# A 1x1 memset instead of a no-operation ahead of each indirect addition of GpSimd

## The chip, the cores and the metric

One core of a Trainium2 chip runs the whole kernel. The metric is the device time of one execution in microseconds (us); a verdict compares medians of several executions. The engines are TensorE (PE, with its weight loads PEld), VectorE (DVE), ScalarE (ACT), GpSimd (POOL) and SyncE (SP), which only issues transfers here.

## The reference

The input is x (4 sequences of 3584 positions, 192 channels), 14336 tokens in all. First comes a causal convolution whose seven weights differ for every position and head and are a softmax over the seven taps:

```
w   = softmax(weight_gen, over 7 taps)          # 4 x 3584 x 8 heads x 7
a   = sum over k of w[..., h, k] * x_pad[s + k, head h]
```

Then a mixture of 8 experts on the 14336 rows `a`: noisy logits from two small products, the two largest of eight, softmax over these two, and for each chosen expert

```
out[row] += top2_w * (relu(a[row] @ w1[e]) @ w2[e])   # 192 -> 1024 -> 192
```

So every output row is the sum of two experts' rows, and these are added where they lie.

## The kernel before, in words

The tokens are cut into 14 chunks of 1024. For each chunk VectorE does the convolution (`conv`, L323 and L333 are its products and sums), ScalarE and VectorE split the rows into two float16 parts in a record buffer `rec` (`split`, L344 and L348), SyncE transposes them for the gate product (L370), and `routing` finds each token's two experts and its place in their queues. GpSimd then writes the records of the chunk to the queues in DRAM (`xg`) by 16 indirect DMAs of 128 rows each (`scatters`, `scatter`, L406 and L407: a 1x1 memset of the tile `spacer`, and the DMA).

Expert work runs in 15 rounds, 14 with blocks of 256 rows for each of the 8 experts and one with blocks of 128. For a round SyncE reads the rows' gates (`meta`, L794) and the transposed rows (`xT`, L800) from the queues (`prologues`). TensorE computes the first product of a block in steps of 512 columns (`mm1`, L856), ScalarE takes its relu (`hi`, L871), VectorE the float16 rest (`lo`, L875), TensorE the second product (`mm2`, L896). `finish` then scales the result into a buffer y on ScalarE (L908; there are six such buffers, four at first) and adds it into the output with an indirect DMA of GpSimd (L913): one addition for each 128 rows, 232 in all. An addition of one block waits until those of the block before have landed.

Nothing of the order is left to chance at run time: each engine has one queue, in the order in which a planner (`Sched`) emits the instructions. Every piece of work is a generator that yields the engine, a duration in us, the function that emits the instruction, and what it depends on. The planner keeps for each engine the time at which it is free. In `step` it takes the earliest piece that could start, and among the pieces of the same engine that could start within 0.3 us of it the one of highest priority. The duration only moves the planner's clock. The pieces this change touches or meets are

- the scatters: duration 1.5, priority 5;
- the additions: duration 1.4, priority 7.5, not before 2.0 us after y is planned to be ready;
- the first and second product: 1.09 and 1.04 for a step, four steps in a block of 256 rows;
- `T["add", n]` and `T["added", bi]`, the planner's times for a free buffer y and for a landed addition, which hang on the addition's planned end, and `T["queued", c]`, which hangs on the last scatter's and lets a round's loads be planned.

A loop at the end (`leftovers`) treats what the rounds left, with a no-operation and an addition of its own.

Of the kernel before, what the change touches and what calls it, by code (L numbers as in the profile page):

```python
# [36 lines left out]
ROUNDS = [(c, 256) for c in range(NC)] + [(NC - 1, 128)]  # L37
# [12 lines left out]
GL, AL, ML, UL, XL = 5.0, 2.0, 5.0, 15.0, 6.0  # L50
# [93 lines left out]
def moe_kernel(ctx, tc, x_lay, wgen, noise, wgn, w1, w2, xg, out):  # L144
    nc = tc.nc
# [27 lines left out]
    def act(n):  # L173
        return (n / 1.2 + 190) / 1e3
# [35 lines left out]
    spacer = const.tile([1, 1], F32, name="spacer")  # L210
# [21 lines left out]
    def before(key, i, n):  # L232

        return [(key, i - n)] if i >= n else []
# [518 lines left out]
    added = []  # L753
# [6 lines left out]
    for c, (_, b) in enumerate(ROUNDS):  # L760
        for e in range(E):
            o = Block()
# [5 lines left out]
    meta, gate_of, token = {}, {}, {}  # L768
# [130 lines left out]
    def finish(bi, t0):  # L899

        o = blist[bi]
        mine = []
        for t in range(o.nt):
            y = []

            def scale():
                y.append((blk if v < 4 else late[1]).tile([P, D], F32, name=f"y{v}", bufs=1))
                nc.scalar.activation(y[0], o.py[t // 2][:, (t % 2) * D:(t % 2 + 1) * D], AF.Copy,  # L908
                                     scale=gate_of[o.c][:, o.e, t:t + 1])

            def add():
                nc.gpsimd.nop()
                i = nc.gpsimd.indirect_dma_start(  # L913
                    out=out, out_offset=bass.IndirectOffsetOnAxis(ap=token[o.c][:, o.e, t:t + 1], axis=0),
                    in_=y[0], in_offset=None, compute_op=OP.add)
                for p in mine:
                    tc.declare_no_dep(i.ins, p.ins, reason="a token has one row in an expert's queue")
                mine.append(i)
                added.append(i)

            n = adds[0]
            adds[0] += 1
            v, u = take(ylast, YB if late else 4, n)
            ty = yield ("ACT", act(D) + 0.07, scale, [t0, ("g", o.c, o.e)] + ([("add", u)] if u is not None else []))
            if t == o.nt - 1:
                T["y", bi] = ty
            ta = yield ("POOL", 1.4, add, [ty + (AL if o.c else 0.0), ("clear", ROUNDS[o.c][0]), ("token", o.c)] + before("added", bi, 1), 0.27)
            T["add", n] = ta + 2.2
        T["added", bi] = ta + 2.6
        if o.e == E - 1:  # L930
            T["round", o.c] = ta + 2.6
# [4 lines left out]
    def take(last, n, user):  # L936

        v = min(range(n), key=lambda i: last.get(i, -1))
        u = last.get(v)
        last[v] = user  # L940
        return v, u
# [4 lines left out]
    def tensor():  # L946
# [3 lines left out]
        def second():  # L950
            sj = pend.pop(0)
            bj, s = steps[sj]
            o = blist[bj]
            deps = [("lo", sj), ("low2", o.e)] + (before("y", bj, 2) if s == 0 else [])
            T["mm2", sj] = t = yield ("PE", 1.04 * o.nf * o.b / 512, lambda: mm2(sj), deps)
            if s == o.n - 1:
                sch.spawn(finish(bj, t), 7.5)
# [155 lines left out]
```

## Time and profile before

| | us |
|---|---|
| median of 3 runs | 1298.4 (1297.04 to 1300.36) |
| the profiled execution | 1293.18 |
| its span, first to last instruction | 1291.4 |
| TensorE busy | 1101.0 |
| VectorE busy | 813.7 |
| GpSimd busy | 731.2 |
| ScalarE busy | 549.6 |

Busy times are those of one profiled execution. A group of instructions is a source line (L913), an engine, what it writes and reads, a count, the busy time and the mean of one. Idle time in front of an instruction is given with what released it; that is inferred from semaphore events. The granted clock (PEclk) is TensorE's, as a share of full speed.

### The profile page before, as it was taken

The page shows a single profiled execution, that of the slowest core. Times are in us where ns is not written, and L with a number is a line of the kernel's source. Part 1 is how long each engine was busy: PE and PEld are TensorE (multiplying, and loading weights), DVE is VectorE, ACT ScalarE, POOL GpSimd, SP SyncE. Part 2 cuts the span into 40 slices and gives each one's busy share as a digit, 9 for nine tenths or more (in the row PEclk, how much of TensorE's full clock was granted, in tenths as well). Part 3 has the DMA queues.
Part 4 walks back from the last instruction along what each step waited for, and adds up shares of the span by engine and source line. Part 5 has one row for each costly group of instructions (what it writes and reads, how often), then busy time and mean ns, then how long its engine had stood idle before and what let it go on. Part 6 is the DMA issues. An engine that isn't in the chain of part 4 may idle for free.

```text
span 1291.4 us, 27931 instructions
## 1 busy us (share of the span) xinstructions
PE 1101.0 (85%) x10958; PEld 975.8 (76%) x10958; DVE 813.7 (63%) x1540; ACT 549.6 (43%) x1231; POOL 731.2 (57%) x781
## 2 busy tenths in 40 slices
PE   0267999999969979889869889969799999999994
PEld 0033677988968969678859879869688889999994
DVE  5447858778868878677858778858644533333331
ACT  6587774444424334324333434323323333333331
POOL 0025165475876847658466574867756777333332
PEclk9998998999999999889989999989898999999997
DMA  9952585537536475455564737546273544334331
GB/s 254 300 164 57 113 203 81 124 75 142 111 58 147 125 98 125 75 104 128 89 126 73 144 65 137 113 60 101 51 102 68 89 82 78 45 50 48 38 39 20
DMA packets 249686, 132.49 MB, mean 103 GB/s; under 512 B 182096, under 2 KB 242000, under 8 KB 247888
## 3 DMA queue, kind: packets, MB, share of 16 engines
q1 hardware_dynamic: 205392, 85.37, 30.3%
q0 software_dynamic: 44160, 45.31, 22.5%
q8 instruction: 86, 1.41, 0.5%
q14 instruction: 48, 0.39, 0.1%
HBM read 38.70 MB, written 58.10 MB: 75 GB/s over the span
## 4 chain that ended last, share of the span: by engine, by line
PE 67%; issue 7%; DMA 7%; ACT 5%; DVE 5%; POOL 4%; SPq 3%; another core or an unknown queue 1%; ACTq 0%; POOLq 0%; DVEq 0%
PE pm L856 34%; PE py L896 29%; POOL xg L407 3%; DMA out<-y,token 2%; PE sums L715 2%; ACT junk L269 2%; DMA xt<-x_lay 2%; SPq L794 1%; POOL out L913 1%; DVE acc L333 1%; DVE tmp L323 1%; DMA xg<-rec,pos 1%; SPq L370 1%; DMA xT<-xg 1%
## 5 line engine op out<-in xcount | busy, mean ns | idle before, releaser
L856 PE MATMUL pm<-xT,wres 128*128 128x256 f16 (+1 forms) x4800 | 601.9, 273 | 27.9 <-DMA xT<-xg 17.9
L913 POOL DMA_INDIRECT out<-y,token x232 | 407.6, 1757 | 364.5 <-ACT y L908 175.2
L896 PE MATMUL py<-wres,hi 128*128 128x192 f16 x3712 | 509.7, 249 | 48.7 <-ACT y L908 18.4
L875 DVE SCALAR_TENSOR_TENSOR lo<-pm,hi 128x512 f16<-128x512 f32 x464 | 316.5, 687 | 345.6 <-ACT hi L871 282.5
L856 PEld LDWEIGHTS <-wres 128*128 128x128 f16 x4800 | 455.5, 99 | 85.6 <-issue 21.5
L871 ACT ACTIVATE hi<-pm 128x512 f16<-128x512 f32 x464 | 275.5, 596 | 568.8 <-PE pm L856 454.4
L896 PE MATMUL py<-wres,lo 128*128 128x192 f16 x1856 | 461.9, 249 | 17.0 <-DVE lo L875 10.5
L896 PEld LDWEIGHTS <-hi 128*128 128x128 f16 x3712 | 343.8, 99 | 71.0 <-issue 39.9
L407 POOL DMA_INDIRECT xg<-rec,pos x224 | 281.3, 1256 | 78.8 <-issue 52.4
L896 PEld LDWEIGHTS <-lo 128*128 128x128 f16 x1856 | 183.7, 99 | 21.1 <-DVE lo L875 13.7
L333 DVE TENSOR_TENSOR acc<-acc,tmp 128x1536 f32<-128x1536 f32 (+1 forms) x90 | 147.9, 1643 | 0.9
L323 DVE TENSOR_TENSOR tmp<-xt,wt 128x1536 f32<-128x1536 f32 (+1 forms) x90 | 147.8, 1643 | 0.7
L908 ACT ACTIVATE y<-py,gate 128x192 f32<-128x192 f32 x232 | 95.5, 418 | 67.0 <-PE py L896 41.5
L406 POOL MEMSET spacer<- 1x1 f32 x224 | 63.5, 283 | 0.1
L715 PE MATMUL sums<-wres,dg 128*128 128x512 f32 (+1 forms) x96 | 53.2, 639 | 7.6 <-ACT wres L719 5.9
L269 ACT ACTIVATE junk<-xt 128x192 f16<-128x192 f32 x118 | 42.7, 362 | 21.9 <-DMA xt<-x_lay 18.6
L529 POOL TENSOR_SCALAR rec<-rr 128x8 f32<-128x8 f32 x14 | 4.5, 319 | 80.4 <-DVE rr L478 79.5
L348 DVE TENSOR_TENSOR rec<-acc,rec 128x512 f16<-128x512 f32 (+2 forms) x30 | 26.8, 898 | 31.8 <-ACT rec L344 31.1
L719 ACT ACTIVATE wres<-sums 128x512 f16<-128x512 f32 (+1 forms) x64 | 34.1, 541 | 25.7 <-PE sums L716 21.2
L715 PEld LDWEIGHTS sums<-wres,dg 128*128 128x128 f32 x96 | 18.2, 215 | 28.2 <-ACT wres L719 17.8
L377 PE MATMUL bank<-wga,xtg 128*128 128x32 f16 x224 | 15.1, 180 | 24.9 <-DMA xtg<-rec 24.5
L598 PE MATMUL sums<-ss,ones 128*128 128x2 f32 x32 | 6.9, 313 | 34.5 <-ACT junk L678 28.0
(132 smaller groups left out, 510.6 us busy)
## 6 DMA issues: line engine op xcount, KB each, us to landing
xt<-x_lay SPq DMA_DIRECT2D x13, 1344.0 KB
out<-zrec SPq DMA_DIRECT2D x14, 768.0 KB
wres<-w SPq DMA_DIRECT2D x6, 768.0 KB
out<-y,token POOLq DMA_INDIRECT x232
xg<-rec,pos POOLq DMA_INDIRECT x224
wt<-wgen SPq DMA_DIRECT2D x14, 224.0 KB
wres<-w SPq DMA_DIRECT2D x6, 512.0 KB
wres<-w SPq DMA_DIRECT2D x12, 256.0 KB
```

Source lines behind the costliest of these rows:

```text
L269: nc.scalar.activation(q, xtile[s][:, i - first], AF.Square, accum_out=nrm[:, i:i + 1])
L323: V.tensor_mul(tm[key].rearrange("p j (h g) -> p j h g", h=H), xt[:, t:t + n].rearrange("p j (h g) -> p j h g", h=H), w[:, a:a + n].rearra ...
L333: ta = yield ("DVE", cc, lambda: V.tensor_add(tm["acc"], tm["acc"], tm["tmp"]), [])
L406: nc.gpsimd.memset(spacer, 0.0)
L407: i = nc.gpsimd.indirect_dma_start(out=xg, out_offset=bass.IndirectOffsetOnAxis(ap=idx, axis=0), in_=src, in_offset=None)
L715: nc.tensor.matmul(o, dg[:, i], w[:, a:a + n], start=True, stop=False)
L856: nc.tensor.matmul(dst, w[:, c0:c0 + 128], m, start=i == 0, stop=i == 4)
L871: nc.scalar.activation(h[0][:, :n], pm[:, :n], AF.Relu)
L875: T["lo", si] = yield ("DVE", dve(n), lambda: nc.vector.scalar_tensor_tensor(h[1][:, :n], pm[:, :n], 0.0, h[0][:, :n], op0=OP.max, op1=OP. ...
L896: nc.tensor.matmul(dst, h[:, cols], w[:, c0:c0 + D], start=begin, stop=f == F // P - 1 and i == 2, skip_group_check=True)
L908: nc.scalar.activation(y[0], o.py[t // 2][:, (t % 2) * D:(t % 2 + 1) * D], AF.Copy, scale=gate_of[o.c][:, o.e, t:t + 1])
L913: i = nc.gpsimd.indirect_dma_start(out=out, out_offset=bass.IndirectOffsetOnAxis(ap=token[o.c][:, o.e, t:t + 1], axis=0), in_=y[0], in_off ...
```

## The change

The no-operation that `finish` puts ahead of each addition becomes a memset of the 1x1 tile `spacer`, as the scatters have it. The planner's duration for an addition, with what stands ahead of it, is raised from 1.4 to 1.85. The loop in `leftovers` keeps its no-operation.

```diff
             def add():
-                nc.gpsimd.nop()
+                nc.gpsimd.memset(spacer, 0.0)
                 i = nc.gpsimd.indirect_dma_start(
                     out=out, out_offset=bass.IndirectOffsetOnAxis(ap=token[o.c][:, o.e, t:t + 1], axis=0),
                     in_=y[0], in_offset=None, compute_op=OP.add)
@@
-            ta = yield ("POOL", 1.4, add, [ty + (AL if o.c else 0.0), ("clear", ROUNDS[o.c][0]), ("token", o.c)] + before("added", bi, 1), 0.27)
+            ta = yield ("POOL", 1.85, add, [ty + (AL if o.c else 0.0), ("clear", ROUNDS[o.c][0]), ("token", o.c)] + before("added", bi, 1), 0.27)
             T["add", n] = ta + 2.2
```

## Rows read from the trace of the kernel before

**Rows 1.** The page: busy time of each engine, share of the span, instructions.
```profile
PE 1101.0 (85%) x10958; PEld 975.8 (76%) x10958; DVE 813.7 (63%) x1540; ACT 549.6 (43%) x1231; POOL 731.2 (57%) x781
```

**Rows 2.** Busy time by stretch: stretch, length, PE, PEld, DVE, ACT, POOL, PEclk, DMA, GB/s.
```profile
0.00:100.00 100.00, 31.64 (x103) 15.45 (x103) 53.87 (x133) 69.89 (x181) 13.56 (x41) 1.00 0.85 234
...
1100.00:1200.00 100.00, 100.00 (x1059) 94.55 (x1057) 34.10 (x56) 37.51 (x73) 37.71 (x27) 1.00 0.39 48
1200.00:1272.00 72.00, 72.00 (x921) 70.00 (x920) 23.89 (x37) 27.43 (x53) 27.09 (x21) 1.00 0.28 35
1272.00:1291.40 19.40, 0.92 (x12) 0.69 (x9) 0.67 (x4) 0.42 (x1) 4.44 (x3) 0.62 0.16 17
```

**Rows 3.** The page's costliest groups, GpSimd's: busy us, mean ns | idle before, releaser.
```profile
L913 POOL DMA_INDIRECT out<-y,token x232 | 407.6, 1757 | 364.5 <-ACT y L908 175.2
...
L407 POOL DMA_INDIRECT xg<-rec,pos x224 | 281.3, 1256 | 78.8 <-issue 52.4
...
L406 POOL MEMSET spacer<- 1x1 f32 x224 | 63.5, 283 | 0.1
```

**Rows 4.** TensorE in order of time, behind its gaps: start, us, what [idle before <-releaser].
```profile
307.22 0.39 PE L856 MATMUL pm<-xT,wres 128*128 128x256 f16 x2 [1.31 <-DMA xT<-xg]
...
373.65 0.34 PE L896 MATMUL py<-wres,hi 128*128 128x192 f16 x2 [1.88 <-ACT hi L871]
...
385.81 1.46 PE L856 MATMUL pm<-xT,wres 128*128 128x256 f16 x6 [8.36 <-DMA xT<-xg]
...
675.19 0.48 PE L896 MATMUL py<-wres,hi 128*128 128x192 f16 x2 [11.50 <-ACT y L908]
...
862.21 0.50 PE L896 MATMUL py<-wres,hi 128*128 128x192 f16 x2 [9.31 <-ACT hi L871]
...
933.47 0.50 PE L896 MATMUL py<-wres,hi 128*128 128x192 f16 x2 [7.14 <-ACT hi L871]
```

**Rows 5.** Who waited for whom (us, times, longest), and ScalarE's wait at 372.69.
```profile
SPq L794 <- DMA xg<-rec,pos: 8.9, 1, 8.9
...
ACT rec L344 <- DMA xg<-rec,pos: 22.8, 2, 12.9
...
372.69 0.42 ACT L908 ACTIVATE y<-py,gate 128x192 f32<-128x192 f32 x1 [6.15 <-DMA out<-y,token]
```

**Rows 6.** GpSimd in order of time, in two stretches.
```profile
369.05 1.61 POOL L913 DMA_INDIRECT out<-y,token  x1 [0.30 <-issue]
370.97 1.57 POOL L913 DMA_INDIRECT out<-y,token  x1 [0.30 <-issue]
371.97 0.61 POOL L406 MEMSET spacer<- 1x1 f32 x1
372.85 0.99 POOL L407 DMA_INDIRECT xg<-rec,pos  x1 [0.26 <-issue]
...
666.00 0.96 POOL L407 DMA_INDIRECT xg<-rec,pos  x1 [0.22 <-issue]
666.95 0.09 POOL L406 MEMSET spacer<- 1x1 f32 x1
667.26 0.96 POOL L407 DMA_INDIRECT xg<-rec,pos  x1 [0.23 <-issue]
668.53 1.61 POOL L913 DMA_INDIRECT out<-y,token  x1 [0.30 <-issue]
```

**Rows 7.** GpSimd's last two additions.
```profile
1276.06 1.54 POOL L913 DMA_INDIRECT out<-y,token  x1 [2.70 <-DMA out<-y,token]
1280.26 1.54 POOL L913 DMA_INDIRECT out<-y,token  x1 [2.65 <-DMA out<-y,token]
```

**Rows 8.** Scatters (L407) alone in one batch: stretch, length, POOL busy (count), PEclk, DMA, GB/s.
```profile
328.10:376.50 48.40, 23.68 (x16) 1.00 0.42 87
```

**Rows 9.** Additions (L913) alone in the same batch, same columns.
```profile
328.10:376.50 48.40, 16.68 (x8) 1.00 0.42 87
```

**Rows 10.** Busy time by stretch, columns as in rows 2, behind the gap at 385.81.
```profile
386.00:390.00 4.00, 4.00 (x26) 3.33 (x25) 1.80 (x7) 0.60 (x1) 0.78 (x2) 0.59 1.19 160
```

## The prediction

> **What bounds the kernel now.** I read the page's busy line first: TensorE is busy for 1101.0 of 1291.4 us, GpSimd for 731.2 [rows 1]. The reader is to see next where TensorE's other 190 us lie, so I cut the span into stages [rows 2]. The first 100 us hold 68 us of them (loading and weight scaling) and the end after 1272 us holds 18. From 1100 to 1272 us TensorE is never idle: the rounds that are left are all fed by then. So some 104 us lie between 100 and 1100 us, in the stage where routing, scattering and expert work run together. An idle microsecond there that is not saved up elsewhere arrives at the end in full, since the saturated last stage can't catch up.
>
> Then the costliest GpSimd groups [rows 3]: 232 additions into the output (L913, 1757 ns each), 224 scatters into the queues (L407, 1256 ns) and a memset ahead of each scatter (L406, 283 ns). Last, I looked at what TensorE's long gaps wait for [rows 4] and followed each to its releaser on ScalarE and the DMA queue [rows 5]. Four of the gaps hang on GpSimd having been late. At 385.81 the new round's rows (xT) are late by 8.36 us because SyncE's queue stood 8.9 us for a scatter. At 862.21 and 933.47 ScalarE has stood (22.8 us in two waits, 12.9 the longer) for the buffer `rec` that a scatter still reads, with the relus behind it in its queue. At 373.65 ScalarE stood 6.15 us for a buffer y that an addition still held. So GpSimd, at 57% over the span, decides time only in stretches: in its batches of 16 scatters.
>
> **The change, first part: a memset in place of the no-operation, 232 times.** The no-operation has no row. What stands where it is can be read: an addition right behind a scatter starts 0.31 us after its end (667.26 + 0.96, then 668.53), and one right behind an addition also 0.31 us (369.05 + 1.61, then 370.97) [rows 6]. Where a memset stands in that place ahead of a scatter, the same two distances are 0.30 us (666.00 + 0.96, memset at 666.95, next start 667.26) and 0.31 us (370.97 + 1.57, memset from 371.97, scatter at 372.85). The memset behind an addition starts 0.57 us before that addition's row ends and lies beside it. So the exchange costs nothing that these rows can show: at their rounding of 0.01 us it is 232 x 0.01 = 2.3 us of GpSimd's time in all. Bounds: below, -0.30 us per addition, if the whole distance were the no-operation's; above, +0.31 us, if the memset came on top of it. I take the 0.01, since it is the same engine, the same kind of DMA behind it and the same two neighbours. Nearly all of it is hidden: the memset waits for nothing and nobody reads what it writes, so it runs while the addition behind it still waits for y or for an earlier addition. That cover holds at the end too, where the additions follow each other at 4.20 us (1276.06, 1280.26) because each waits 2.65 us for the one before to land [rows 7]. In a batch with no idle time it is not hidden: 8 additions by 0.01 us, nothing; at the upper bound 8 x 0.31 = 2.5 us.
>
> The Trainium skill (Perfetto Trace Analysis, GPSIMD Engine Instruction) says that a GpSimd instruction's span is not to be trusted and that one should take the spacing of starts. By the span of L406 (283 ns) the 232 memsets would be 66 us of GpSimd's time; by the spacing, which the sum uses, 2.3 us. The rows bear the rule out here: the memset's span is 0.09 us behind a scatter and 0.61 us behind an addition, and the distance is 0.31 us both times.
>
> **Second part: the planner's duration for an addition goes from 1.4 to 1.85.** This is what can move the time, for the kernel's order on every engine is written out by this planner. Real spacing: an addition takes 1.757 + 0.30 = 2.06 us, a scatter 1.256 + 0.31 = 1.57 us on average [rows 3, 6]. So the old number is 0.66 us too small and the new one 0.21. In a saturated batch 8 additions stand among the 16 scatters; it takes 48.4 us, with 16.7 us of additions and 23.7 us of scatters busy [rows 8, 9]. The planner reckons 16 x 1.5 + 8 x 1.4 = 35.2 us for it, so the plan runs ahead of the chip by 13 us at the batch's end: that is the lateness behind the four gaps.
>
> What a larger number does to the order: an addition has the higher priority (7.5 against 5 for a scatter). A block of 256 rows takes 88 matmuls, and 1059 of them run in 100 us, so 12 blocks, 8.3 us each [rows 2]; the planner's own block is 4 x (1.09 + 1.04) = 8.5 us. It has two additions. Before, they leave 8.5 - 2.8 = 5.7 us, 3.8 scatters; after, 8.5 - 3.7 = 4.8 us, 3.2 scatters. Sixteen scatters then span 5.0 blocks instead of 4.2, with 10 additions among them instead of 8.4, so 1.6 more stand ahead of the last scatter: 1.6 x 2.06 = 3.3 us later on the chip, and about 7 us later in the plan (42.5 against 35.2 to 36).
>
> Which waits that moves: two round starts wait on xT with nothing in hand (307.22 and 385.81) [rows 4]; there 3.3 us more of scattering are 3.3 us more of idle TensorE, 6.6 together. The two gaps on `rec` see the scatter later too, but also a plan that places ScalarE's waiting copy later; the one offsets the other, and I book nothing. The y wait gets an earlier addition; its gap on TensorE is 1.88 us, and I book nothing as well, because the granted clock behind a new gap costs about as much: in the 4 us behind the gap at 385.81 it is 0.59 [rows 10], near the 1.2 GHz level, so some 1.6 us of work are lost.
>
> Sum: the profiled execution took 1293.18 us (span 1291.4 and 1.8 around it). 1293.2 + 0 + 6.6 = 1299.8. The runs' median, 1298.4, stands 5.2 us above it, so on the median the forecast is 1305.0 us. Its own range is 1302 (one boundary) to 1314 (four boundaries and the clock behind them).
>
> **Rivals.** *The truer plan wins.* The plan's lead over the chip in that batch shrinks from 13 to about 10 us (two more additions: 42.5 us planned, 48.4 + 2 x 2.06 = 52.5 on the chip). For it: the gaps at 373.65, 675.19 (behind ScalarE's scaling, 11.50 us), 862.21 and 933.47 are ScalarE stuck in an order that believed GpSimd done [rows 4, 5]; it decides once the four shrink by these 3 us, 12 us together, against the 6.6 above. Against it: the real additions and scatters vary with what runs beside them (a scatter takes 23.7 / 16 = 1.48 us on average in that batch against 0.96 at best) [rows 6, 8], which no planned number follows. Time: 1298.4 - 12 = about 1286 us, 1280 to 1294.
>
> *Nothing that can be measured.* GpSimd's order in a batch changes by one or two places, gaps move from one round to another, and the sum stays. For it: GpSimd has 16 x (2.06 + 1.57) = 58 us of work in a round of eight blocks that takes TensorE 8 x 8.3 = 67 us, so it has slack outside the batches. Against it: the order of all engines is drawn anew from one number, and the gaps of [rows 4] depend on it. Time: 1298.4, within 0.3% (3.9 us), which is about what a measurement of this kernel can tell from no change.
>
> *The memset costs its full distance.* Not slower through the plan but directly: 8 x 0.31 = 2.5 us per saturated batch; if five batches are as full as that of [rows 8], 12 us, 1311 us. It decides from the point where GpSimd is never idle in a batch. Against it: the two distances above. It is part of the slower chance.
>
> *The change does nothing that it says*: no, the memset will have 232 rows.
>
> **How the numbers follow.** Scatters later (my forecast), 0.39; memset at its full distance, 0.05; truer plan, 0.31; nothing measurable, 0.25. So slower by over 0.3% 0.44, faster 0.31, within 0.3% 0.25. The cases of both signs hold most of the chance, so the range reaches from the middle of the truer plan to beyond the four boundaries with a memset at full distance: 1283 to 1319 us.
>
> **What would show it.** L913 should have 232 new memset rows, 0.09 us behind a scatter and 0.6 behind an addition, with the distances from end to next start still 0.3 us. The batches of 16 scatters should hold 9 or 10 additions and last 3 us longer. xT should release TensorE's gaps at the round starts more often, and ScalarE's waits on `rec` and y should be shorter. The forecast is wrong if TensorE's idle time between 100 and 1100 us falls below 104 us; then the truer plan has won. If the distance in front of an addition grows to 0.6 us, the first part was mispriced.

## The result, and the profile after

The changed kernel takes 1311.3 us (median of 11 runs, 1299.1 to 1317.7) where the kernel before takes 1295.2 (11 runs, 1291.1 to 1300.4) in the same comparison: a ratio of 1.011, with a 95% interval of 1.0076 to 1.0143, so 10 to 19 us slower. The forecast was 1305.0 us, on a median of 1298.4, that is 6.6 us slower. The direction is right and the size under half (6.6 us for 16.1). The mechanism that carried the 6.6 us is not the one that acted.

The page of the kernel after, busy line and groups (columns as in [rows 1] and [rows 3]):

```profile
PE 1101.5 (84%) x10958; PEld 981.0 (75%) x10958; DVE 815.6 (62%) x1540; ACT 549.8 (42%) x1231; POOL 743.5 (57%) x1013
...
L913 POOL DMA_INDIRECT out<-y,token x232 | 410.4, 1769 | 372.7 <-ACT y L908 176.1
...
L407 POOL DMA_INDIRECT xg<-rec,pos x224 | 280.1, 1251 | 74.5 <-issue 51.9
...
L912 POOL MEMSET spacer<- 1x1 f32 x232 | 89.6, 386 | 0.1
```

The reader is to see that nothing is dearer than it was. The additions take 1769 ns for 1757, the scatters 1251 for 1256 [rows 3]. GpSimd's busy time grows by 12 us, not by the 89.6 us of the new group, since most of a memset's span lies beside the addition ahead of it. So the time came in through idle engines. By stretch, first the kernel before in the two stretches that [rows 2] doesn't hold, then the kernel after (columns as in [rows 2]):

```profile
100.00:1100.00 1000.00, 896.39 (x8870) 795.14 (x8871) 701.20 (x1313) 414.31 (x926) 648.38 (x691) 0.95 0.54 101
```

```profile
0.00:100.00 100.00, 29.21 (x97) 14.53 (x97) 48.96 (x131) 64.75 (x173) 9.21 (x35) 1.00 0.89 231
100.00:1100.00 1000.00, 883.74 (x8710) 786.41 (x8711) 702.81 (x1307) 413.97 (x923) 652.30 (x872) 0.95 0.54 101
...
1288.60:1312.20 23.60, 0.00 (x0) 0.00 (x0) 0.67 (x4) 0.42 (x1) 5.06 (x7) 0.57 0.17 19
```

TensorE's idle time between 100 and 1100 us rises from 103.6 to 116.3 us, 12.7 more. The end, in which only additions run, grows from 18.5 us of idle TensorE (19.40 less 0.92 busy [rows 2]) to 23.6, 5.1 more. The first 100 us hold 2.4 more, and TensorE is busy for 0.5 more: 20.7 of the 20.8 us between the two profiled spans (1291.4 and 1312.2). These two executions lie a little further apart than the medians (16.1 us). The 2.4 us of the start are hardly the change's: no addition stands there, and a later kernel with the old duration (landing 3.05) idles as long (71.0 us; before 68.4, after 70.8).

Who TensorE waited for (us in total, times, longest), before:

```profile
PE py L896 <- ACT y L908: 18.4, 4, 11.5
PE py L896 <- ACT hi L871: 18.3, 3, 9.3
PE py L896 <- issue: 18.0, 29, 4.2
PE pm L856 <- DMA xT<-xg: 17.9, 4, 8.4
PE py L896 <- DVE lo L875: 10.5, 7, 4.5
```

and after:

```profile
PE py L896 <- ACT y L908: 52.0, 26, 9.5
...
PE pm L856 <- DMA xT<-xg: 11.7, 3, 6.9
PE bank L500 <- DVE th L492: 11.5, 3, 7.0
PE py L896 <- issue: 8.2, 14, 1.7
...
PE py L896 <- DVE lo L875: 4.0, 5, 1.5
PE py L896 <- ACT hi L871: 3.8, 2, 3.5
```

The small net hides large terms of both signs. The second product's waits for ScalarE's scaling of y (which frees its PSUM bank `py`) grow by 33.6 us, from 4 waits to 26. Those on xT, `hi` and `lo` fall by 6.2, 14.5 and 6.5. The rest are waits at small products of routing (L500, 10.8 more) and weights, and 14.6 us less of "issue".

The shape of the y waits is plain on ScalarE in the saturated stage. The kernel before, ScalarE in order of time, its scalings:

```profile
1199.80 0.42 ACT L908 ACTIVATE y<-py,gate 128x192 f32<-128x192 f32 x1 [0.39 <-PE py L896]
1203.47 0.41 ACT L908 ACTIVATE y<-py,gate 128x192 f32<-128x192 f32 x1
```

The kernel after:

```profile
1198.86 0.73 ACT L908 ACTIVATE y<-py,gate 128x192 f32<-128x192 f32 x2 [0.44 <-PE py L896]
...
1207.14 0.73 ACT L908 ACTIVATE y<-py,gate 128x192 f32<-128x192 f32 x2 [0.39 <-PE py L896]
```

Before, a block's second y follows its first by 3.67 us. After, two scalings run together every 8.3 us. The first of the two is the one released by a product that has just ended, so it is the first y of a block, and the one behind it is the second y of the block before. That second one thus comes more than a whole block late (8.65 us behind the first of its own block, median over the 112 blocks of 256 rows, paired by the order in the code; before 3.67), and holds `py` until then. A scaling placed that late shares ScalarE's queue with whatever stands ahead of it. At the longest such gap ScalarE stood for a scatter; ScalarE and then TensorE, after:

```profile
782.91 1.48 ACT L344 ACTIVATE rec<-acc 128x1536 f16<-128x1536 f32 x1 [6.97 <-DMA xg<-rec,pos]
784.30 0.41 ACT L908 ACTIVATE y<-py,gate 128x192 f32<-128x192 f32 x1
```

```profile
784.76 0.48 PE L896 MATMUL py<-wres,hi 128*128 128x192 f16 x2 [9.52 <-ACT y L908]
```

Before, a copy to `rec` of this kind held up a relu [rows 4, 5]; now it holds up a y.

### The profile page after: what moved, and what is told of

It is laid out like the page before. It is cut to its first block, busy times and chain, and to the rows that moved or that the text cites. A ratio compares the mean times of both kernels' runs of the same rounds, so it can differ in the third digit from the quotient of the medians.

```text
span 1312.2 us, 28128 instructions
## 1 busy us (share of the span) xinstructions
PE 1101.5 (84%) x10958; PEld 981.0 (75%) x10958; DVE 815.6 (62%) x1540; ACT 549.8 (42%) x1231; POOL 743.5 (57%) x1013
## 4 chain that ended last, share of the span: by engine, by line
PE 57%; POOL 13%; DMA 10%; ACT 6%; issue 6%; SPq 4%; DVE 2%; another core or an unknown queue 1%; DVEq 0%; ACTq 0%; POOLq 0%
PE pm L856 28%; PE py L896 26%; POOL xg L407 7%; POOL out L913 5%; DMA xt<-x_lay 3%; DMA wres<-w 2%; PE sums L715 2%; ACT junk L269 2%; SPq L370 2%; SPq L794 2%; DMA xg<-rec,pos 1%; DMA out<-y,token 1%; ACT y L908 1%; ACT hi L871 1%
## 5 line engine op out<-in xcount | busy, mean ns | idle before, releaser
L913 POOL DMA_INDIRECT out<-y,token x232 | 410.4, 1769 | 372.7 <-ACT y L908 176.1
L856 PE MATMUL pm<-xT,wres 128*128 128x256 f16 (+1 forms) x4800 | 599.0, 273 | 16.9 <-DMA xT<-xg 11.7
L407 POOL DMA_INDIRECT xg<-rec,pos x224 | 280.1, 1251 | 74.5 <-issue 51.9
L908 ACT ACTIVATE y<-py,gate 128x192 f32<-128x192 f32 x232 | 90.1, 419 | 50.5 <-PE py L896 43.6
L912 POOL MEMSET spacer<- 1x1 f32 x232 | 89.6, 386 | 0.1
L406 POOL MEMSET spacer<- 1x1 f32 x224 | 64.4, 288 | 0.1
L719 ACT ACTIVATE wres<-sums 128x512 f16<-128x512 f32 (+1 forms) x64 | 34.1, 542 | 24.4 <-PE sums L716 23.6
```

The lines of the kernel that those rows point to most:

```text
L407: i = nc.gpsimd.indirect_dma_start(out=xg, out_offset=bass.IndirectOffsetOnAxis(ap=idx, axis=0), in_=src, in_offset=None)
L856: nc.tensor.matmul(dst, w[:, c0:c0 + 128], m, start=i == 0, stop=i == 4)
L912: nc.gpsimd.memset(spacer, 0.0)
L913: i = nc.gpsimd.indirect_dma_start(out=out, out_offset=bass.IndirectOffsetOnAxis(ap=token[o.c][:, o.e, t:t + 1], axis=0), in_=y[0], in_off ...
```

## The experiments

A ratio is the kernel's time over that of the kernel before in the same comparison, with its 95% interval. The kernel before took 1263.0 us beside the first four, 1292.4 beside the next four and 1265.5 beside the last four, so only ratios are compared across them.

**The two parts alone, and the change again.**

```diff
# memset alone: duration stays 1.4
-                nc.gpsimd.nop()
+                nc.gpsimd.memset(spacer, 0.0)
```

> The memset with the planner's number left at 1.4: the order on TensorE, VectorE, ScalarE and SyncE is that of the kernel before, GpSimd has 232 memsets more. Theory A (the planner's number costs, the memset nothing): ratio to before 1.000, within 0.997 to 1.003, and the distance from one GpSimd DMA to the next stays 0.30 us. Theory B (the memset costs by itself, in GpSimd's full batches and in the chain of additions at the end): 1.005 to 1.011, and the additions of the last round follow each other at 4.28 us instead of 4.20.

```diff
# plan alone: the no-operation stays
-            ta = yield ("POOL", 1.4, add, ...
+            ta = yield ("POOL", 1.85, add, ...
```

> The no-operation kept, the planner's number 1.85: the changed kernel's order without its memsets. Theory A: ratio to before 1.008 to 1.014, all of what the change costs. Theory B: 0.997 to 1.003. If both have a share, the two ratios of this run and of the memset alone multiply to 1.011.

The changed kernel, a second time:

> The changed kernel once more, for a second profile of it. Its first profile reaches the first scatter 5.0 us later than that of the kernel before, ahead of any piece that the change touches. If that belongs to the change (a longer instruction stream, or the order of the loads), the first scatter starts near 92 us again; if it is the execution's own scatter, it starts near 87 us, and the ratio to before is 1.007 to 1.012 all the same.

Memset alone: 1.0000 (0.9959 to 1.0041). Plan alone: 1.0023 (0.9993 to 1.0054). Both: 1.0052 (1.0010 to 1.0094). The memset costs nothing that can be measured. What there is of a loss goes with the duration, though here the plan alone is not told apart from no change. That is a miss for the expectation of the plan alone, which had 1.008 or more if the number costs; only its waits show the cost here (41.4 us for y, without a memset). With both parts the ratio is smaller than the first 1.011, and the intervals meet only between 1.0076 and 1.0094.

The profiles of memset alone, which has the order of before, and of the change again stand in one comparison. From the first to the second TensorE's waits for y go from 9.3 to 44.2 us, and those on xT, `hi` and `lo` together from 71.7 to 23.9: the same exchange as in the first pair. But its idle time between 100 and 1100 us falls here, from 95.5 to 87.3, while the end grows from 18.7 to 23.5. So the exchange repeats, and the 12.7 us of the first pair do not. The first scatter starts at 91.6 us in the second profile of the change (92.3 in the first), at 87.3 and 90.3 in the two of the kernel before, and at 92.3 with landing 0.8 and the old duration, so no part of that start is shown to be the change's.

The distances agree. Memset alone, GpSimd in order of time:

```profile
603.57 1.48 POOL L407 DMA_INDIRECT xg<-rec,pos  x1 [0.22 <-issue]
605.05 0.09 POOL L912 MEMSET spacer<- 1x1 f32 x1
605.36 1.61 POOL L913 DMA_INDIRECT out<-y,token  x1 [0.22 <-issue]
606.35 0.66 POOL L912 MEMSET spacer<- 1x1 f32 x1
607.27 1.87 POOL L913 DMA_INDIRECT out<-y,token  x1 [0.26 <-issue]
```

An addition starts 0.31 us behind a scatter's end (605.05 to 605.36) and 0.30 us behind an addition's (606.97 to 607.27): the 0.31 of the no-operation [rows 6].

**More of the suspected cost.**

```diff
-                nc.gpsimd.nop()
+                nc.gpsimd.memset(spacer, 0.0)
+                nc.gpsimd.memset(spacer, 0.0)
+                nc.gpsimd.memset(spacer, 0.0)
+                nc.gpsimd.memset(spacer, 0.0)
```

> Four memsets ahead of each addition, planner's number 1.4 as before: the direct cost made visible by its dose. Theory A: three memsets more are 0.09 us each behind a scatter and hidden behind an addition that waits; 8 additions in a full batch by some 0.3 us are 2 to 3 us a batch at most, ratio 1.000 to 1.006. Theory B: four times the share of the single memset, 1.02 or more.

Measured: 1.0324 (1.0257 to 1.0392), far above what theory A had and inside what theory B had, though memset alone speaks against B. GpSimd in order of time:

```profile
626.92 0.96 POOL L407 DMA_INDIRECT xg<-rec,pos  x1 [0.22 <-issue]
627.88 0.09 POOL L912 MEMSET spacer<- 1x1 f32 x1
628.03 0.09 POOL L913 MEMSET spacer<- 1x1 f32 x1
628.17 0.09 POOL L914 MEMSET spacer<- 1x1 f32 x1
628.32 0.09 POOL L915 MEMSET spacer<- 1x1 f32 x1
629.13 1.61 POOL L916 DMA_INDIRECT out<-y,token  x1 [0.72 <-issue]
```

The addition now starts 1.25 us behind the scatter's end where one memset left 0.31; elsewhere in the same stretch it is 0.69. So three further memsets cost 0.4 to 0.9 us, and this reaches the end: some 41 us, while the 14 batches of scatters, first start to last end, last 598 us in sum. With one memset and the same order they last 557, so the batches are 41 us longer too: lateness of GpSimd that the plan doesn't know was paid about one for one here. Of the 38.7 us between these two profiles 25.5 are idle TensorE (209.0 for 183.5), and 13.2 are longer busy time, at a mean granted clock of 0.945 for 0.959. That the single memset is free is therefore, as far as this dose tells, a matter of its price and not of cover.

**Is it the late rounds, or the memset in them?** GpSimd's last additions lag further behind the last product in the changed kernel, so three kernels were aimed there.

The kernel before, a second time:

> The kernel before, unchanged, for a profile of it beside the other runs of this chip. Ratio 1.000. Theory T (at the end the two kernels differ by the chain of additions): the last addition starts 7.3 us after TensorE's last matmul, as in its first profile, against 11.5 in both profiles of the changed kernel and 9.4 with the plan alone; and TensorE's last matmul ends within 4 us of where it does with the plan alone (1250.9). Theory M (the middle costs): TensorE's last matmul ends 6 us or more earlier than there, near 1243 or below.

```diff
# late price: 1.85 in the last two rounds only, no-operation
-            ta = yield ("POOL", 1.4, add, ...
+            ta = yield ("POOL", 1.4 if o.c < NC - 1 else 1.85, add, ...
```

> No-operation, 1.4 for every addition but those of the last two rounds, which are planned at 1.85; the order up to the last two rounds is that of the kernel before. Theory T: if the late order alone makes the lag, the last addition starts 9.4 us after the last matmul and the time is 2 us longer, ratio 1.001 to 1.003. If the lag was set by the order that earlier rounds left, it stays 7.3 and the ratio is 1.000. Theory M: 1.000 either way.

```diff
# the changed kernel, no-operation in the last two rounds
+                nc.gpsimd.memset(spacer, 0.0) if o.c < NC - 1 else nc.gpsimd.nop()
```

> The changed kernel, but the no-operation in place of the memset for the 24 additions of the last two rounds. Theory T: the last addition starts 9.4 us after the last matmul, as with the plan alone, and the one long step of 5.7 us in the chain of the last round is gone; ratio to before 1.002 to 1.004 against 1.005 of the changed kernel. If the memsets of the earlier rounds matter, the time stays at 1.005; if the long step has nothing to do with the memset, the lag stays at 11.5.

The kernel before again: 1.0008 (0.9973 to 1.0042). Late price: 0.9988 (0.9951 to 1.0025), so the late rounds alone don't make the loss. No memset late: 1.0109 (1.0071 to 1.0146), the ratio of the change, so the memset at the end doesn't make it either. From the last product's end to the last addition's start it is 7.7, 8.2 and 10.3 us in these three; the last was expected at 9.4 or 11.5 and lies between. The long step in its chain of additions shrinks from 5.7 to 4.6 us. Where the last product ends can't be compared with the 1250.9 us of the expectation, since that was taken in the faster comparison.

**A price that is true.**

```diff
-            ta = yield ("POOL", 1.4, add, ...
+            ta = yield ("POOL", 2.06, add, ...
```

> No-operation, planner's number 2.06, the spacing that the trace of before shows for an addition. Theory of the truer plan (a number nearer the chip's gives a better order): at or below before, 0.990 to 1.000. Theory of my forecast (a longer addition pushes the scatters back, systematically): worse than 1.85 with the no-operation, 1.005 to 1.012. Theory of the draw (each number gives another order, good or bad, with no trend): anything within 0.99 to 1.015 and not between the others.

Measured: 1.0417 (1.0357 to 1.0477). With the spacing that the trace gives, the loss is 4.2%, where 1.85 cost 0.5 to 1.1%. That is above the range of all three theories, and GpSimd's occupation alone can't explain it. TensorE's waits for y are 101.6 us.

That led to another theory. `finish` takes a block's steps one after the other: first y, first addition, second y, second addition, and the next block's first addition not before `T["added", bi]`, 2.6 us behind the planned landing of this block's second. The duration stands in this chain too. Worked out from the code, a block's planned chain is 2.62 us from the first addition to the second (scaling 0.42, 0.2, and 2.0 of margin, if the second scaling is planned where the first addition starts), then the duration, 0.7 + 0.27 + 0.9 + 0.2 of landing, and 2.6: 8.69 us at 1.4, 9.14 at 1.85, 9.35 at 2.06. It can be shorter, where the plan has ScalarE free before the first addition starts, but the two additions are never less than one duration apart, so it is at least 7.47, 8.37 and 8.79. The planned products of a block take 8.52. Where the chain comes out longer than the products, the planned additions fall behind from block to block, and the second y, planned behind the first addition, falls behind with them. On the chip an addition needs no such margin: in the last round, with one addition a block, they follow each other at 4.20 us [rows 7], where the plan has 6.07 at 1.4 (4.67 and the duration).

This theory says that the same chain with another duration acts alike, which "the duration as occupation" denies. So the landing was moved, with the duration held, in both directions.

```diff
# landing 2.15: the changed kernel, chain as before the change (8.69)
-        T["added", bi] = ta + 2.6
+        T["added", bi] = ta + 2.15
```

> The changed kernel (memset, 1.85), but the planner's time for a landed block of additions is the last addition's plus 2.15 instead of 2.6, so that block-to-block it reckons what it did before the change. Theory C (the planner's chain of additions: second addition at least 2.6 us behind the first, then 1.4 + 4.67 = 6.07 to the next block's first, 8.69 us a block against 8.52 for the products; with 1.85 it is 9.14 and the chain falls behind by 0.62 us a block, so the second scaling slips behind the next block's and TensorE waits for it): the chain is 8.69 again, TensorE's waits on ScalarE's y fall from some 50 us to 10 to 30, ratio to before 0.997 to 1.004. Theory P (the longer occupation of GpSimd in the plan, which pushes the scatters back): nothing changes, ratio 1.005 to 1.012, waits on y stay near 50 us.

```diff
# landing 3.05: the kernel before, chain as in the changed kernel (9.14)
-        T["added", bi] = ta + 2.6
+        T["added", bi] = ta + 3.05
```

> The kernel before (no-operation, 1.4) with plus 3.05 instead of 2.6: the planner's chain of additions is that of the changed kernel, GpSimd's occupation that of before, and there is no memset. Theory C: ratio 1.005 to 1.014 and 40 to 60 us of TensorE's waits on y, like the change. Theory P: 0.997 to 1.003, waits on y 10 to 26 us.

```diff
# landing 0.8: the changed kernel, chain 7.34
-        T["added", bi] = ta + 2.6
+        T["added", bi] = ta + 0.8
```

> The changed kernel (memset, 1.85) with plus 0.8: the planner reckons 1.85 + 2.87 = 4.72 us from one block's last addition to the next block's first, near the 4.3 that the chip takes, so 7.3 us a block, below the products' 8.52. Theory C: the second scaling no longer slips, waits on y under 15 us, and the time is at or below before, 0.985 to 1.002, memsets and all. Theory P: 1.005 to 1.012.

```diff
# old price 0.8: the kernel before, chain 6.89
-        T["added", bi] = ta + 2.6
+        T["added", bi] = ta + 0.8
```

> The kernel before (no-operation, 1.4) with plus 0.8: 6.9 us a block in the plan. Theory C: waits on y under 15 us where before has 18 to 26, time 0.985 to 1.000; a version that could beat both kernels. Theory P: no change beyond another draw of the order, 0.995 to 1.005. Between this run and the one with 1.85 and plus 0.8 stand the memset and GpSimd's occupation alone.

| duration | landing | planned chain, us: least, and with 2.62 | last product ends in the plan, us | ratio (95%) | y waits of TensorE, us | second y behind the first, us |
|---|---|---|---|---|---|---|
| 1.4 | 0.8 | 5.67; 6.89 | 1213.0 | 0.9985 (0.9957 to 1.0013) | 1.0 | 1.58 |
| 1.85 | 0.8 | 6.57; 7.34 | 1216.3 | 0.9783 (0.9740 to 0.9825) | 3.0 | 1.63 |
| 1.4 | 2.6 (before) | 7.47; 8.69 | 1220.0 | 1 | 18.4; 26.3; 9.3 with the memset | 3.67 |
| 1.85 | 2.15 | 7.92; 8.69 | 1225.6 | 0.9830 (0.9779 to 0.9881) | 24.6 | 5.80 |
| 1.4 | 3.05 | 7.92; 9.14 | 1270.0 | 1.0446 (1.0410 to 1.0483) | 92.6 | 8.70 |
| 1.85 | 2.6 (the change) | 8.37; 9.14 | 1243.6 | 1.011; 1.0052 the second time | 52.0; 44.2 | 8.65; 8.64 |
| 2.06 | 2.6 | 8.79; 9.35 | 1309.0 | 1.0417 (1.0357 to 1.0477) | 101.6 | 10.68 |

The fourth column is not measured: it is the planner's own clock, as the code of each kernel gives it. TensorE's waits for y in memset alone, plan alone, landing 2.15, landing 3.05 and with 2.06, in this order:

```profile
PE py L896 <- ACT y L908: 9.3, 5, 4.0
...
PE py L896 <- ACT y L908: 41.4, 19, 9.4
...
PE py L896 <- ACT y L908: 24.6, 11, 7.8
...
PE py L896 <- ACT y L908: 92.6, 32, 12.7
...
PE py L896 <- ACT y L908: 101.6, 62, 6.2
```

Theory C had the y waits in its ranges in three of the four runs (landing 3.05 went beyond), and the time in one: landing 2.15 and 0.8 came out faster than it said and 3.05 slower. Theory P had the y waits of neither landing 2.15 nor 3.05, and the time only of the old price with 0.8, where the two theories meet.

TensorE's longest waits with landing 0.8 and the new duration, and its wait for y:

```profile
PE pm L856 <- DMA xT<-xg: 47.3, 8, 8.4
...
PE py L896 <- ACT y L908: 3.0, 2, 2.0
```

With landing 0.8 and the old duration:

```profile
PE py L896 <- DVE lo L875: 37.4, 8, 9.4
...
PE pm L856 <- DMA xT<-xg: 30.2, 5, 9.2
```

Two things follow. First, the y waits and the late second y go with the planned chain and not with the duration or the memset: the plan alone has them without a memset, and so has the old duration with a landing 0.45 longer. At either duration the time rises with the landing. But the first 20 us of y waits cost next to nothing (0.983 for 0.9783, 1 for 0.9985). In landing 3.05 ScalarE shows the pairs of the changed kernel:

```profile
1197.67 0.73 ACT L908 ACTIVATE y<-py,gate 128x192 f32<-128x192 f32 x2 [0.39 <-PE py L896]
```

Second, with the chain held the larger duration is a gain: 0.983 against 1 at 8.69, and with the short landing 0.9783 against 0.9985. (At 9.14 it is 1.0052 or 1.011 against 1.0446, but these are of different comparisons and the plans are not equally long.) The planner's clock tells the two terms apart. In the kernels of the table, beside the kernel before, the measured ratio is that of the planned ends within 0.5% for 1.4, lies 0.8 to 2.2% below it for 1.85, and 2.9% below it for 2.06. So the change was a gain of about 2% and a loss of about as much (1.9% by the planned ends, 1243.6 for 1220.0; 2.3% from 0.983 to 1.0052, across two comparisons), and only their difference was measured. That the gain comes because the plan knows better how long GpSimd is busy is argued: no run shows by which wait it comes. Landing 0.8 with the new duration takes the gain alone: 1238.7 us against 1265.5, 2.2% (1.75 to 2.6) faster than the kernel before, which the changed kernel is not.

What the experiments leave open. Each kernel's order is drawn anew, so a part of any one ratio may be chance; the steps of 4% in the table and the y waits are much larger than the 0.1% of the late price, which also redrew an order, though only of two rounds. Why the landing of 0.8 gains nothing with the old duration is open: it waits 37.4 us for `lo` where the new duration waits 6.3, but less on xT (30.2 against 47.3). And it is open why the change costs 1.1% beside one kernel before (1295 and 1292 us) and 0.5% beside another (1263).

## Why the prediction was half right

The range of 1283 to 1319 us holds the 1311.3, but it reaches from the truer plan to a dear memset, so that says little. That the sign came out is luck: the waits that were to grow fell, and a wait that the sum had at nothing grew by more.

**The memset at 0.01 us an addition: right, its cover wrong.** The distances of 0.30 and 0.31 us, the 232 rows, and the spans of 0.09 us behind a scatter and 0.6 behind an addition came as predicted. The kernel after, GpSimd in order of time:

```profile
599.10 0.96 POOL L407 DMA_INDIRECT xg<-rec,pos  x1 [0.23 <-issue]
600.04 0.09 POOL L912 MEMSET spacer<- 1x1 f32 x1
600.36 1.61 POOL L913 DMA_INDIRECT out<-y,token  x1 [0.23 <-issue]
601.35 0.66 POOL L912 MEMSET spacer<- 1x1 f32 x1
```

The Trainium skill (Perfetto Trace Analysis, GPSIMD Engine Instruction) had it that such spans are not to be trusted. This case bears it out to the end: 232 such spans, 89.6 us of them in the kernel after, are worth a ratio of 1.0000 (0.9959 to 1.0041) in memset alone. The rival with the memset at its full distance falls by the same run. But "nearly all of it is hidden" was hardly what made it free. With three more memsets the time followed at 41 us. That is 0.47 us for each of the 87 additions that stand among scatters in the kernel before, so it is as if all batches counted, and not the five full ones of that rival.

**More additions ahead of the last scatter: the sign right, the size not.** The prediction had 1.6 more in a batch and 3.3 us. In the 14 batches the additions among the scatters went from 87 to 93, half a one for each of the 12 that hold more than one. The batch of [rows 8, 9], in the kernel after, scatters and then additions alone (columns as there):

```profile
331.60:382.90 51.30, 22.90 (x16) 1.00 0.51 106
...
331.60:382.90 51.30, 18.90 (x8) 1.00 0.51 106
```

It is 2.9 us longer, but with the same 8 additions, each of which took 2.36 us instead of 2.09. All 14 batches last 606 us for 561, 3.2 each; in the second run of the change 570, for 557 in memset alone, 1.0 each. So the lengthening came, mostly not through the order that was to cause it. Nor does a fuller batch cost time by itself: landing 2.15 and 0.8 with the new duration have 95 and 99 additions among the scatters and 570 and 575 us of batches, and are the two fastest kernels; landing 3.05 has 73 and 528 us, and is 4.5% slower than before.

**Two xT gaps, +6.6 us: the step that failed.** Waits on xT fell from 17.9 to 11.7 us (from 27.1 to 12.6 between memset alone and the change again); they were to rise. A later scatter in the plan also moves what the plan places behind it, so a longer batch is not a longer wait. The prediction made that argument for `rec` and not for xT.

**The `rec` gaps booked at nothing: a gain missed.** TensorE's waits for `hi` fell by 14.5 and for `lo` by 6.5 us. ScalarE's waits to write `rec` itself fell only from 22.8 [rows 5] to 20.5. This is the rival "the truer plan wins", and it was right in its own part: it priced the gain at 12 us, and the pair at an equal chain gives 1.7%, some 21 us.

**The y wait booked at nothing: the loss missed.** It was +33.6 us, and that is what showed in place of the xT term. The prediction foresaw an earlier addition and so an earlier free buffer y; it looked at the buffers and not at the bank `py`, which the scaling itself frees, nor at where the plan puts the second scaling. What would have shown it was in its hands: `T["added"]` stands among the planner's times that hang on the addition's end, the sum of 9.14 us against 8.52 can be made before any run, and so can the planner's own end, 1243.6 us for 1220.0. A price in this planner is two things, how long GpSimd is taken and how late everything behind it is. Only the first was weighed.

**The end: "that cover holds at the end too".** The memset is covered there, but the end grew all the same. The kernel after, GpSimd's additions in the last stretch:

```profile
1277.38 1.56 POOL L913 DMA_INDIRECT out<-y,token  x1 [2.64 <-DMA out<-y,token]
...
1283.04 1.56 POOL L913 DMA_INDIRECT out<-y,token  x1 [4.06 <-ACT y L908]
...
1287.29 1.56 POOL L913 DMA_INDIRECT out<-y,token  x1 [2.64 <-ACT y L908]
...
1300.18 1.56 POOL L913 DMA_INDIRECT out<-y,token  x1 [2.71 <-DMA out<-y,token]
```

The steps are 4.2 to 4.4 us, near those of [rows 7], but for one of 5.66 (1277.38 to 1283.04). The y that it adds, by the order in the code, had been scaled by 1274.42, so the releaser in that row is not what held it. The last addition starts 11.6 us behind the last product (1288.6), before it was 7.3 [rows 7]; with the plan alone 9.4, with the landing at 0.8 and the new duration 5.5. Most of the lag stands before the long step: the last addition of the blocks of 256 rows, whose second y is scaled late like the others, starts 24.3 us ahead of the last product's end instead of 27.0. In the order of the change the long step goes with the memset (5.66 and 5.70 with it, 4.56 without it in the last rounds, 4.27 with the plan alone), but landing 3.05 has one of 5.57 without any memset. What places it is open.

**"Wrong if TensorE's idle time between 100 and 1100 us falls below 104".** It rose to 116.3, as the forecast needed, and for another reason; in the second comparison it fell from 95.5 (memset alone) to 87.3, and the kernel was no faster. A sum of idle time can bear out a forecast whose terms are wrong; only the waits by releaser told them apart.

## What to carry to other kernels

Where a planner's duration feeds both an engine's free time and a chain of due times, change the two apart: raise the duration to what the trace shows, and take the same amount out of the margin behind it. Then compare the planned length of the chain for one unit of work with that of the engine that bounds, and read the planner's own end before any run: a chain that is longer falls behind with every unit, and what it drags along may be an operation that frees something else. When a large change of order moves the time little, list the waits by releaser on both sides before believing that little happened.

## What the runs showed of the hardware

A memset of one element between two indirect DMAs costs nothing over a no-operation (0.30 to 0.31 us either way, and a ratio of 1.0000), but three more cost 0.4 to 0.9 us, though each has a span of 0.09.

The same kernel took 1263 and 1265.5 us in two of the comparisons and 1292 in the third, over 2% apart. The three ran on three different chips. In the profiles of the slower one TensorE has many short gaps inside its blocks that wait for nothing the profile shows; the kernel before, a second time:

```profile
PE py L896 <- issue: 13.2, 28, 1.0
...
PE pm L856 <- issue: 7.7, 18, 1.0
```

They add up to 11 to 28 us in the six profiles of kernels that ran at that level, and none of the other eight has one at these lines. What makes them is open. Between the profile of memset alone and this one TensorE's idle time grows by 13.0 us (183.5 to 196.5) and its busy time by 12.5 (1082.7 to 1095.2), so the gaps are not the whole of the difference.
